# Attention units in pairs, a second tile of queries, and the fourth accumulator copy in another ring

## The chip, the cores and the metric

The kernel runs on one core of one Trainium2 chip. The metric is the device time of one execution in microseconds; shorter is better. Times are given as a median of several executions, and one more execution is recorded by the hardware profiler.

## The reference

The input is attention in chunks (batch 4, 8 heads, 768 positions, head dimension 64), whose output feeds two matrix layers. Cut to what matters:

```
chunk, left_ctx, right_ctx = 32, 16, 8           # every chunk also sees 8 memory keys
scores = (q_c @ k_full^T) / sqrt(64)             # per chunk, 64 keys
a      = exp(scores - max);  a = a / (sum(a) + 1e-9)
x      = a @ v_full                              # 3072 tokens x 512
x      = leaky_relu(x @ w_in, 0.01) @ w_out      # 512 -> 2048 -> 512   (first layer pair)
out    = ((x @ w_a) * (x @ w_b)) @ w_out2        # 512 -> 1536 -> 512   (second layer pair)
```

All data are float32. Each big product is three matmuls over parts: a factor is split into a rounded part (xh, gh, the first half of w) and the rest (xl, gl, the second half), and low by high, high by low and high by high are added up.

## The kernel before

The 3072 tokens are cut into 24 attention units of 128 tokens, and into six blocks of 512 tokens, so four units make a block. The list SEQ gives the order of the units.

One unit has these steps. Its scores are 32 matmuls of 64 columns into a PSUM tile s of the ring "s" (L279, function a_scores). ScalarE (ACT) places the queries of a later unit into the tile qz (L251, L252, q_place). VectorE (DVE) takes the maximum and subtracts it, ACT takes the exponential, DVE divides and transposes (L293 to L348). The product with V is 32 more matmuls of 64 columns into a tile pv of the same ring "s" (L388, a_pv). That ring has two buffers. The tile pv is then read: for units of blocks 0 to 3 by a_out, which casts it to xh on ACT (L421) and lets DVE subtract it again for xl (L422), and for units of blocks 4 and 5 by a_raw, which is one copy on ACT (L405 or L408).

Beside the attention runs the first layer pair, as items (block, f), where f is one of 16 slices of the hidden layer. One item is mm1 (12 matmuls of 512 columns into h, L435 to L437), leaky relu and split on ACT and DVE (g, gh, gl; L527, L530, L533), and mm2 of an earlier item (12 matmuls into the four accumulators a of the block, L559 to L563). After the last f of a block the four accumulators are copied by ACT to tiles x (the ring "z", three buffers) and stored to x2d (L576, L577). Blocks 4 and 5 follow in another form (products A, B, C with sums u and s in the rings "t" and "z"; their functions record all at L49). The second layer pair takes the rest of the time, from about 600 us.

A third strand prepares the weights of the second layer pair during blocks 1 to 3: raw words are loaded (raw<-w, L704), scaled by ACT (L106), joined by DVE (L116, L119), combined (ps, L755), split by ACT and DVE (tiles pwa and pwb, L125 and L126) and stored again (wab, wtd).

The order is fixed by hand and by the scheduler. The list STARTS holds, for each unit from the ninth on, the number of the item at which its scores are issued; its softmax, transposes and product with V follow at the next three items. The scheduler then fixes one order for each engine. Each engine works through its own order strictly, and SyncE (SP) issues the DMAs in its order. Weights w are loaded by wo_load into the ring "wo" of six buffers, which the second part of each item reads.

Of the kernel before, what the change touches and what calls it, by code (L numbers as in the profile page):

```python
# [7 lines left out]
F32 = mybir.dt.float32  # L8
# [6 lines left out]
P = 128  # L15
B, H, S, D = 4, 8, 768, 64
CH, LEFT, RIGHT, NMEM = 32, 16, 8, 8
WIN = LEFT + CH + RIGHT
UT = 128
# [7 lines left out]
TB = 512  # L27
NB3 = NT // TB
NL = NB3 - 2
SEQ = list(range(12)) + [16, 12, 13, 14, 15] + list(range(17, NU))  # L30


class InOrder:
# [22 lines left out]
def kernel(  # L56
# [144 lines left out]
    att = tc.tile_pool(name="att", bufs=4, side="left")  # L201
    ap_ = att.__enter__()
    ident = sm.tile([P, P], F32, tag="id", name="id", bufs=1)
    qz = ap_.tile([P, 16, 2 * CH], F32, tag="qz", name="qz", bufs=1)
    qs = [
        prep.tile([P, 2 * CH, 16], F32, tag=t, name="qs", bufs=1) for t in ("pz", "ps", "pwa", "pwb")
    ]
# [11 lines left out]
    for t in qs[2:4]:  # L219
        nc.gpsimd.memset(t[0:64, CH:2 * CH, :], 0.0)  # L220
        nc.gpsimd.memset(t[64:128, 0:CH, :], 0.0)
    nc.gpsimd.memset(qz[0:64, :, CH:2 * CH], 0.0)
    nc.gpsimd.memset(qz[64:128, :, 0:CH], 0.0)

    kt, vt, st, qr = {}, {}, {}, {}
    qu, ku, vu = [[a[u] for u in SEQ] for a in (q_l, k_l, v_l)]
# [3 lines left out]
    def q_load(upto):  # L230
        while loaded[0] < min(upto, NU):
            u = loaded[0]
            if u < len(qs):
                eng = act if u < 1 else sp
                sp.dma_start(out=qs[u][0:64, 0:CH, :], in_=qu[u][0:64])
                eng.dma_start(out=qs[u][64:128, CH:2 * CH, :], in_=qu[u][64:128])
            else:
                t = ap_.tile([P, CH, 16], F32, tag="qr", name="qr", bufs=2)
                sp.dma_start(out=t, in_=qu[u])
                qr[u] = t  # L240
            loaded[0] += 1

    def q_of(u):
        return qs[u].rearrange("p q o -> p o q") if u < len(qs) else qz

    def q_place(u, copy):
        if u >= NU:
            return
        t = qr.pop(u).rearrange("p q o -> p o q")
        qb = qz  # L250
        copy(qb[0:64, :, 0:CH], t[0:64])  # L251
        copy(qb[64:128, :, CH:2 * CH], t[64:128])  # L252

    def k_load(upto):
        while loaded[1] < min(upto, 2 * NU):
            u, cp = divmod(loaded[1], 2)
            t = ap_.tile([P, 512], F32, tag="k", name="k")
            sp.dma_start(out=t, in_=ku[u][cp])
            kt[u, cp] = t
            loaded[1] += 1  # L260
# [282 lines left out]
    def mm2(bi, parts, g):  # L543
        if bi not in acc:
            last = bi == NB3 - 1
            acc[bi] = [
                p.tile([P, TB], F32, tag=t, name="a")
                for p, t in (((ps_h, "h"), (ps_s, "s")) * 2 if last else ((ps_a, "a"),) * KC)
            ]
        gh, gl = g  # L550
        for o, n, f in parts:
            slot = wslot[f, 1]
            t = slice(o, o + n)
            for e in range(KC):
                ps = acc[bi][e][:, t]
                c = slice(e * P, e * P + P)

                kw = dict(skip_group_check=bi == 0)
                pe.matmul(  # L559
                    ps, slot[:, 1, c], gh[:, t], start=f == 0 and o == 0, stop=False, **kw  # L560
                )
                pe.matmul(ps, slot[:, 0, c], gl[:, t], start=False, stop=False, **kw)  # L562
                pe.matmul(  # L563
                    ps, slot[:, 0, c], gh[:, t], start=False,
                    stop=f == NF1 - 1 or (o == HALF and f == LEAD - 1), **kw
                )
            if bi == 0:
                ready = {(0, NF1 - 1): slice(0, HALF), (HALF, LEAD - 1): slice(HALF, TB)}
                t = ready.get((o, f))
            else:  # L570
                t = t if f == NF1 - 1 else None
            if t is not None:
                for e in range(KC):
                    ps = acc[bi][e][:, t]
                    y = tp.tile([P, TB], F32, tag="z", name="x2", bufs=3)
                    act.copy(y[:, t], ps)  # L576
                    (act if bi == NB3 - 1 else sp).dma_start(out=x2d[bi][:, e, t], in_=y[:, t])  # L577

# [96 lines left out]
    def at_item(i, *args):  # L675
        at(*divmod(i, NF1), *args)

    STARTS = (17, 20, 23, 26, 29, 32, 34, 37, 39, 42, 44, 47, 50, 52, 54, 57)
    for k, i in enumerate(STARTS):
        u = 2 * TB // UT + k  # L680
        blk, o = divmod(SEQ[u], TB // UT)
        at_item(i, a_scores, u)
        at_item(i, load_qk, u)
        at_item(i, a_soft1, u)
        at_item(i + 1, a_soft2, u)
        at_item(i + 2, a_turn, u)
        at_item(i + 3, a_pv, u, ps_s, "s")
        at_item(i + 3, load_v, u)
        if blk < NL:
            at_item(i + 3, a_out, u, ("x", blk), o * UT)  # L690
        else:
            at_item(i + 3, a_raw, u)

    sources = []
    for p in range(NF2 // 2):
# [151 lines left out]
    def wo_load(upto):  # L847
        while wo_next[0] < upto:
            b, f = 1 + wo_next[0] // NF1, wo_next[0] % NF1
            if b == NB3:  # L850
                break
            t = wop.tile([P, 2, 512], F32R, tag="wo", name="w")
            nc.sync.dma_start(out=t.bitcast(F32), in_=wod[f])
            wslot[f, 1] = t
            wo_next[0] += 1
# [95 lines left out]
            pe.matmul(ps, w[:, 0, c], lo[:, kc], start=False, stop=False, **kw)  # L951
            pe.matmul(ps, w[:, 0, c], hi[:, kc], start=False, stop=kc == hc - 1, **kw)

    at_item(max(STARTS) + 3, y_begin)
    at_item(max(STARTS) + 4, y_subs)
    at_item(max(STARTS) + 5, s_begin)

    STEPS = 58
    for bi, f, parts in items[LEAD:]:
        first = bi == 0  # L960
        if f == 0 and not first:
            if bi + 1 < NL:
                x_tiles(("x", bi + 1))
            else:
                x_raw()
        if first:
            W1.load(2 * f + 14)
            W1.step()
        behind.append((bi, parts, mm1(bi, parts)))
        if first:  # L970
            W1.step()
        if len(behind) > LAG:
            mm2(*behind.pop(0))
        for fn in beside.get((bi, f), []):
            fn()
        if not first:
            wo_load((bi - 1) * NF1 + f + 4)

            i = (bi - 1) * NF1 + f
            n = (NL - 1) * NF1  # L980
            for _ in range(STEPS * (i + 1) // n - STEPS * i // n):
                next(steps, None)
        elif f >= NF1 - 1:
            wo_load(f - NF1 + 2)
            prep_load(f - NF1 + 1)


    def relu(src, kept=None):
        g = tp.tile([P, TB], F32, tag="t", name="g")
        act.activation(g, src, AF.Prelu, alpha=0.01)  # L990
        if kept is None:
            gh = tp.tile([P, TB], F32R, tag="gh", name="gh", bufs=3)
            gl = tp.tile([P, TB], F32R, tag="gl", name="gl", bufs=3)
        else:
            w = wp.tile([P, 2, TB], F32R, tag=f"wi{kept}", name="g5")
            gh, gl = w[:, 0], w[:, 1]
        act.copy(gh, g)

        def low():
            dve.tensor_tensor(out=gl, in0=g, in1=gh.bitcast(F32), op=ALU.subtract)  # L1000
            return gh, gl

        return low
# [3 lines left out]
        act.copy(t, ps)  # L1007
        return t

    def summed(x, y):  # L1010
        t = tp.tile([P, TB], F32, tag="z", name="s", bufs=3)
        dve.tensor_tensor(out=t, in0=x, in1=y, op=ALU.add)
        return t

# [18 lines left out]
    for p in range(NF1 // 2):  # L1033
        f0, f1 = 2 * p, 2 * p + 1
        A = ps_h.tile([P, TB], F32, tag="h", name="A")
        prod(A, p, 0, 0, True)
        Bk = ps_s.tile([P, TB], F32, tag="s", name="B")
        if p:
            act.copy(Bk, A)
            low12 = relu(late, f1 - 2)  # L1040
        else:
            a1 = snapped(A)
            y_part(2)
        next2(behind.pop(0))
        if p:
            kept[f0 - 2] = low12()
        prod(Bk, p, 1, 1, p == 0)
        if p:
            next(steps, None)
        if p and p + 1 < NF1 // 2:  # L1050
            s_sums(p + 1)
        low11 = relu(Bk if p else summed(a1, Bk))
        g11 = low11()
        if not p:
            s_sums(p + 1)
        prod(A, p, 2, 4, False)
        u2 = snapped(A)
        if p == 0:
            y_part(6)
        C = ps_s.tile([P, TB], F32, tag="s", name="C")  # L1060
        prod(C, p, 3, 3, True)
        if p + 1 < NF1 // 2:
            s_parts(p + 1, 0)
            s_parts(p + 1, 1)
        prod(A, p, 4, 5, False)
        u3 = snapped(A)
        s22 = summed(u3, C)
        next2(part2(NL, f0, g11))
        kept[f1] = relu(s22, f0)()
        if p:  # L1070
            next(steps, None)
        prod(A, p, 5, 2, False)
        low21 = relu(A)
        prod(C, p, 6, 6, False)
        behind.append(part2(NL, f1, low21()))
        late = summed(u2, C)
# [520 lines left out]
```

## Time and profile before

| | us |
|---|---|
| three runs | 1123.5, 1125.94, 1125.79 |
| median of these | 1125.79 |
| profiled execution, its own time | 1122.23 |
| span of the profiled execution | 1120.4 |
| PE (TensorE) busy | 1099.6 |
| DVE busy | 774.0 |
| ACT busy | 527.1 |

The span is what the trace covers; the 1.8 us beside it in the profiled execution's own time lie around it. The three runs lie 2.4 us apart.

In the profile, PE is the matmul side of TensorE and PEld its weight loads. A row of the timeline gives the start, the duration, the engine and the line, the operation, and what is written and read; in square brackets stands how long the engine was idle just before and what released it.

### The profile page before, as it was taken

Reading aid. Unit: us, or ns where it says so; the run is one execution under the profiler, and the core shown is the slowest. Engines: PE = TensorE matmul, PEld = TensorE weight load, DVE = VectorE, ACT = ScalarE, POOL = GpSimd, SP = SyncE. Lnnn points to the kernel's source line nnn. Section 1 sums busy time; section 2 is a strip of 40 time slices with the busy share of each in tenths; the row PEclk is TensorE's granted clock in tenths of the full one; section 3 lists DMA queues with packets and bytes.
Section 4 is the critical chain, followed back from the end, with each engine's and each line's share of the span. In section 5 each row is a group of like instructions: output and inputs, shape, how many; then the busy total and the mean of one; then the engine's idle time right before and its main releaser. Section 6 shows DMA issues by size and latency. Waiting matters only on the chain.

```text
span 1120.4 us, 16313 instructions
## 1 busy us (share of the span) xinstructions
PE 1099.6 (98%) x6194; PEld 909.0 (81%) x6194; DVE 774.0 (69%) x1418; ACT 527.1 (47%) x893; POOL 6.3 (1%) x16
## 2 busy tenths in 40 slices
PE   7899999999999999999999999999999999999997
PEld 6788888888887887888888888888888888888886
DVE  6796489988997975777441737588736578745666
ACT  5887555465555535666522434144434243433232
POOL 2000000000000000000000000000000000000000
PEclk9999999999999999999999999999999999999999
DMA  9996789999998953444687756566877576867452
GB/s 312 404 349 228 280 330 325 337 319 312 345 316 312 343 189 132 155 147 141 206 335 248 271 186 206 172 212 196 272 227 222 167 225 190 241 179 244 142 187 76
DMA packets 100526, 271.15 MB, mean 242 GB/s; under 512 B 9696, under 2 KB 24672, under 8 KB 99680
## 3 DMA queue, kind: packets, MB, share of 16 engines
q1 hardware_dynamic: 98704, 268.41, 71.3%
q10 hardware_dynamic: 1744, 1.70, 0.5%
q8 instruction: 49, 0.80, 0.3%
q14 instruction: 29, 0.24, 0.1%
HBM read 215.29 MB, written 54.79 MB: 241 GB/s over the span
## 4 chain that ended last, share of the span: by engine, by line
PE 93%; issue 2%; ACT 2%; DVE 1%; DMA 1%; ACTq 0%; SPq 0%; DVEq 0%
PE ca L49 18%; PE cc L49 9%; PE oa L49 8%; PE a L49 7%; PE h L435 5%; PE h L436 5%; PE h L437 5%; PE a L559 5%; PE a L562 5%; PE a L563 5%; PE cb L49 5%; PE oy L49 4%; PE A L49 4%; PE pv L388 2%; PE C L49 2%
## 5 line engine op out<-in xcount | busy, mean ns | idle before, releaser
L49 PE MATMUL ca<-ch,wab 128*128 128x512 f32 x576 | 192.1, 389 | 0.1
L49 ACT CAST st<-gb 128x512 fp32r<-128x512 f32 x126 | 76.6, 622 | 124.5 <-DVE gb L49 123.9
L49 PEld LDWEIGHTS ca<-ch,wab 128*128 128x128 f32 x576 | 108.1, 188 | 23.3 <-ACT a L49 0.5
L49 PE MATMUL ca<-cl,wab 128*128 128x512 f32 x288 | 112.1, 389 | 0.0
L49 PE MATMUL oa<-st,wt 128*128 128x512 f32 x420 | 104.3, 389 | 0.0
L435 PE MATMUL h<-xh,w 128*128 128x512 f32 (+1 forms) x256 | 101.9, 398 | 0.7 <-ACT xh L49 0.7
L49 PE MATMUL cc<-ch,wab 128*128 128x512 f32 x288 | 100.3, 389 | 0.0
L436 PE MATMUL h<-xl,w 128*128 128x512 f32 (+1 forms) x256 | 98.7, 386 | 0.2 <-DVE xl L49 0.2
L559 PE MATMUL a<-gh,w 128*128 128x512 f32 (+1 forms) x256 | 97.7, 382 | 1.1 <-ACT x L576 1.1
L437 PE MATMUL h<-xh,w 128*128 128x512 f32 (+1 forms) x256 | 98.7, 385 | 0.0
L562 PE MATMUL a<-gl,w 128*128 128x512 f32 (+1 forms) x256 | 97.5, 381 | 0.0
L563 PE MATMUL a<-gh,w 128*128 128x512 f32 (+1 forms) x256 | 97.4, 381 | 0.0
L49 DVE TENSOR_TENSOR st<-gb,st 128x512 fp32r<-128x512 f32 x126 | 85.3, 689 | 14.9 <-ACT st L49 12.5
L49 PEld LDWEIGHTS oa<-st,wt 128*128 128x128 f32 x420 | 78.8, 188 | 16.4
L49 ACT COPY u<-ca 128x512 f32<-128x512 f32 x72 | 42.3, 587 | 91.5 <-PE ca L49 91.3
L348 DVE STREAM_TRANSPOSE pt<-p 32x128 f32<-32x128 f32 x256 | 77.5, 303 | 4.4
L49 PEld LDWEIGHTS cc<-ch,wab 128*128 128x128 f32 x288 | 54.0, 188 | 11.2
L49 PEld LDWEIGHTS ca<-cl,wab 128*128 128x128 f32 x288 | 54.0, 188 | 11.0
L435 PEld LDWEIGHTS h<-xh,w 128*128 128x128 f32 x256 | 48.1, 188 | 11.4 <-ACT xh L49 0.8
L559 PEld LDWEIGHTS a<-gh,w 128*128 128x128 f32 x256 | 48.1, 188 | 10.8 <-ACT x L576 1.5
L533 DVE TENSOR_TENSOR gl<-g,gh 128x512 fp32r<-128x512 f32 (+1 forms) x64 | 43.2, 675 | 18.5 <-ACT gh L530 14.9
L49 PE MATMUL cc<-cl,wab 128*128 128x512 f32 x144 | 56.0, 389 | 0.0
(197 smaller groups left out, 2035.8 us busy)
## 6 DMA issues: line engine op xcount, KB each, us to landing
wab<-wab SPq DMA_DIRECT2D x126, 512.0 KB, 4.4
w<-wod SPq DMA_DIRECT2D x80, 512.0 KB, 5.6
raw<-w SPq DMA_DIRECT2D x68, 512.0 KB, 7.0
wt<-wtd SPq DMA_DIRECT2D x63, 512.0 KB, 4.6
k<-kl SPq DMA_DIRECT2D x48, 256.0 KB, 5.2
v<-vl SPq DMA_DIRECT2D x48, 256.0 KB, 5.3
wab<-pwb SPq DMA_DIRECT2D x12, 768.0 KB, 7.1
wod<-w SPq DMA_DIRECT2D x16, 512.0 KB, 6.5
```

The lines of the kernel that those rows point to most:

```text
L49: self.last = emit(*args, **kwargs).ins
L348: dve.transpose(out=pt[o0:o0 + 32, :, 2 * cpar + hpar, hpx, :], in_=p[i0:i0 + 32, hpx::2, 32 * b:32 * b + 32],)
L388: pe.matmul(o[64 * hpar:64 * hpar + 64, 2 * pair:2 * pair + 2, t0:t0 + CH], v[:, i:i + 64], pt[:, 2 * cp + pair, 2 * cpar + hpar].rearrang ...
L435: pe.matmul(ps, w[1], x[0], start=first, stop=False)
L436: pe.matmul(ps, w[0], x[1], start=False, stop=False)
L437: pe.matmul(ps, w[0], x[0], start=False, stop=last)
L533: dve.tensor_tensor(out=gl[:, c], in0=g[:, c], in1=gh[:, c].bitcast(F32), op=ALU.subtract)
L559: pe.matmul(ps, slot[:, 1, c], gh[:, t], start=f == 0 and o == 0, stop=False, **kw)
L562: pe.matmul(ps, slot[:, 0, c], gl[:, t], start=False, stop=False, **kw)
L563: pe.matmul(ps, slot[:, 0, c], gh[:, t], start=False, stop=f == NF1 - 1 or (o == HALF and f == LEAD - 1), **kw)
```

## The change

Three things change. First, from the ninth unit on, the units go in pairs: the list STARTS has nine places instead of sixteen, and at each place the products with V of one pair are issued in a row, and then the scores of the next pair in a row. Units 16 and 17 of SEQ stand together. Second, a pair needs two tiles of queries: the second qz is taken from the ring "wo" that holds weights, which has five buffers left for weights while the attention runs, so a weight is asked for three items ahead instead of four. Third, for blocks after the first the fourth accumulator copy takes its buffer from the ring "t" and not from "z", and so does the first sum s.

```
-SEQ = list(range(12)) + [16, 12, 13, 14, 15] + list(range(17, NU))
+SEQ = list(range(12)) + [16, 17, 12, 13, 14, 15] + list(range(18, NU))
...
-    qz = ap_.tile([P, 16, 2 * CH], F32, tag="qz", name="qz", bufs=1)
+    qz = [ap_.tile([P, 16, 2 * CH], F32, tag="qz", name="qz", bufs=1)]
...
+    def q_tile(u):
+        return qz[u % 2 if u > 8 else 0]
...
-                    y = tp.tile([P, TB], F32, tag="z", name="x2", bufs=3)
+                    tag, bufs = ("z", 3) if e < KC - 1 or bi == 0 else ("t", None)
+                    y = tp.tile([P, TB], F32, tag=tag, name="x2", bufs=bufs)
...
-    STARTS = (17, 20, 23, 26, 29, 32, 34, 37, 39, 42, 44, 47, 50, 52, 54, 57)
-    for k, i in enumerate(STARTS):
-        u = 2 * TB // UT + k
+    def q_second():
+        qz.append(wop.tile([P, 16, 2 * CH], F32, tag="wo", name="qz"))
+        nc.gpsimd.memset(qz[1][0:64, :, CH:2 * CH], 0.0)
+        nc.gpsimd.memset(qz[1][64:128, :, 0:CH], 0.0)
+        q_place(9, nc.scalar.copy)
+        q_load(12)
+
+    def next_pair(u):
+        for k in (2, 3):
+            q_place(u + k, nc.scalar.copy)
+        q_load(u + 6)
+        k_load(2 * u + 8)
+
+    def out_of(u):
         blk, o = divmod(SEQ[u], TB // UT)
-        at_item(i, a_scores, u)
-        at_item(i, load_qk, u)
+        if blk < NL:
+            a_out(u, ("x", blk), o * UT)
+        else:
+            a_raw(u)
+
+    at(0, NF1 + LEAD - 1, q_second)
+    STARTS = (17, 23, 29, 34, 40, 45, 50, 55, 60)
+    for k, i in enumerate(STARTS[:-1]):
+        u, end = 2 * TB // UT + 2 * k, STARTS[k + 1]
+        for v in (u, u + 1):
+            at_item(end, a_pv, v, ps_s, "s")
+            at_item(end, out_of, v)
+        at_item(end, v_load, 2 * u + 8)
+    for k, i in enumerate(STARTS[:-1]):
+        u = 2 * TB // UT + 2 * k
+        for v in (u, u + 1):
+            at_item(i, a_scores, v)
+        at_item(i, next_pair, u)
         at_item(i, a_soft1, u)
+        at_item(i, a_soft1, u + 1)
         at_item(i + 1, a_soft2, u)
         at_item(i + 2, a_turn, u)
-        at_item(i + 3, a_pv, u, ps_s, "s")
-        at_item(i + 3, load_v, u)
-        if blk < NL:
-            at_item(i + 3, a_out, u, ("x", blk), o * UT)
-        else:
-            at_item(i + 3, a_raw, u)
+        at_item(i + 2, a_soft2, u + 1)
+        at_item(i + 3, a_turn, u + 1)
...
-            wo_load((bi - 1) * NF1 + f + 4)
+            wo_load((bi - 1) * NF1 + f + 3)
...
-    def summed(x, y):
-        t = tp.tile([P, TB], F32, tag="z", name="s", bufs=3)
+    def summed(x, y, tag="z"):
+        t = tp.tile([P, TB], F32, tag=tag, name="s", bufs=3 if tag == "z" else None)
...
-        low11 = relu(Bk if p else summed(a1, Bk))
+        low11 = relu(Bk if p else summed(a1, Bk, "t"))
```

Numbers behind an underscore tell buffers apart; lines of the changed kernel stand a few higher (a_pv L391, a_scores L282, a_out L424 and L425, the accumulator copies L580).

The order of PE in the kernel before, in the second block, where one unit's product with V (pv) ends and the next unit's scores (s) begin:

```order
L563 MATMUL a_1750<-gh_1948,w_1768 128x512
L388 MATMUL pv_2066<-pt1_130,v_1566 64x2x32 x8
L388 MATMUL pv_2066<-pt1_130,v_1568 64x2x32 x8
L279 MATMUL s_2089<-k_1712,qz_124 64x64 x8
L279 MATMUL s_2089<-k_1714,qz_124 64x64 x8
L435 MATMUL h_2129<-xh_375,w_852 128x512
L436 MATMUL h_2129<-xl_376,w_852 128x512
```

One product is followed by one score, and the score takes the buffer that the score before it left.

The order of PE in the changed kernel at the second pair of products, in the same block:

```order
L566 MATMUL a_1787<-gh_2351,w_2262 128x512
L391 MATMUL pv_2448<-pt0_129,v_2088 64x2x32 x8
L391 MATMUL pv_2448<-pt0_129,v_2090 64x2x32 x8
L391 MATMUL pv_2467<-pt1_130,v_2092 64x2x32 x8
L391 MATMUL pv_2467<-pt1_130,v_2094 64x2x32 x8
L438 MATMUL h_2561<-xh_375,w_1268 128x512
L439 MATMUL h_2561<-xl_376,w_1268 128x512
L440 MATMUL h_2561<-xh_375,w_1268 128x512
L282 MATMUL s_2494<-k_2138,qz_124 64x64 x8
L282 MATMUL s_2494<-k_2140,qz_124 64x64 x8
L282 MATMUL s_2511<-k_2142,qz_1607 64x64 x8
L282 MATMUL s_2511<-k_2144,qz_1607 64x64 x8
```

Two products and two scores stand together, with three matmuls of h between them. Both products take a buffer of the ring "s", and both scores take one after them.

The order of ACT in the kernel before at the same place of PE (xh<-pv is the reader of pv, raw and pwb belong to the preparation of the weights):

```order
L527 ACTIVATE g_2048<-h_2035 128x512
L530 CAST gh_2050<-g_2048 128x512
L125 CAST pwb_2234<-ps_2222 128x4x256
L421 CAST xh_1611<-pv_2066 128x4x128
L106 ACTIVATE raw_2124<-raw_2124 128x512
L251 COPY qz_124<-qr_1907 64x16x32
```

The cast of pv stands alone, behind a split of prepared weights.

The order of ACT in the changed kernel at that second pair:

```order
L530 ACTIVATE g_2430<-h_2417 128x512
L533 CAST gh_2432<-g_2430 128x512
L106 ACTIVATE raw_2607<-raw_2607 128x512
L424 CAST xh_1620<-pv_2448 128x4x128
L125 CAST pwa_2977<-pz_2780 128x256
L424 CAST xh_1620<-pv_2467 128x4x128
L125 CAST pwa_2977<-pz_2780 128x256 x2
```

A scaling of raw words now stands ahead of the first cast of pv, and a split of prepared weights between the two casts.

The order of DVE in the changed kernel there, with the second readers (xl<-pv):

```order
L116 TENSOR_SCALAR pz_2780<-raw_2607 128x512
L119 SCALAR_TENSOR_TENSOR pz_2780<-raw_2607,pz_2780 128x512
L783 TENSOR_TENSOR ps_2978<-pz_2780,ps_2978 128x256
L783 TENSOR_TENSOR ps_2978<-pz_2780 128x256
L425 TENSOR_TENSOR xl_1621<-pv_2448,xh_1620 128x4x128
L126 TENSOR_TENSOR pwa_2977<-pz_2780,pwa_2977 128x256
L425 TENSOR_TENSOR xl_1621<-pv_2467,xh_1620 128x4x128
```

A join (pz) and two sums (ps) stand ahead of the first subtraction, and a split of weights between the two.

The order of ACT in the kernel before at the end of block 2, where the accumulators a are copied (gh, in the last row but one, is for mm2):

```order
L576 COPY x2_3900<-a_2807 128x512
L576 COPY x2_3903<-a_2808 128x512
L576 COPY x2_3906<-a_2809 128x512
L125 CAST pwa_4315<-pz_4231 128x256 x3
L527 ACTIVATE g_3956<-h_3943 128x512
L530 CAST gh_3958<-g_3956 128x512
L576 COPY x2_3909<-a_2810 128x512
```

The fourth copy stands behind three splits and behind g and gh of the next item.

The order of ACT in the changed kernel at the end of block 2:

```order
L580 COPY x2_3897<-a_2805 128x512
L580 COPY x2_3900<-a_2806 128x512
L580 COPY x2_3903<-a_2807 128x512
L580 COPY x2_3906<-a_2808 128x512
L125 CAST pwb_4402<-ps_4269 128x4x256
L530 ACTIVATE g_3937<-h_3924 128x512
L533 CAST gh_3939<-g_3937 128x512
```

The four copies now stand in a row, ahead of the next split, g and gh.

## Rows read from the trace of the kernel before

**Rows 1.** The page: the span, and busy times and clock by engine.

```profile
span 1120.4 us, 16313 instructions
...
PE 1099.6 (98%) x6194; PEld 909.0 (81%) x6194; DVE 774.0 (69%) x1418; ACT 527.1 (47%) x893; POOL 6.3 (1%) x16
...
PEclk9999999999999999999999999999999999999999
```

**Rows 2.** Stage 135 to 245 us: length, busy of PE, PEld, DVE, ACT, POOL, clock, DMA.

```profile
135.00:245.00 110.00, 110.00 (x815) 91.24 (x814) 95.45 (x230) 63.31 (x102) 0.00 (x0) 1.00 0.92 320
```

**Rows 3.** What PE waited for, us in total, times, longest; two rows.

```profile
PE A L49 <- ACT u L49: 1.3, 1, 1.3
PE a L559 <- ACT x L576: 1.1, 1, 1.1
```

**Rows 4.** Timeline of PE around a pv and s run, and an s run.

```profile
153.85 0.39 PE L563 MATMUL a<-gh,w 128*128 128x512 f32 x1
154.17 1.15 PE L388 MATMUL pv<-pt,v 128*64 128x64 f32 x32
...
156.18 0.50 PE L435 MATMUL h<-xh,w 128*128 128x512 f32 x1
156.52 0.39 PE L436 MATMUL h<-xl,w 128*128 128x512 f32 x1
...
241.21 0.39 PE L563 MATMUL a<-gh,w 128*128 128x512 f32 x1
241.53 1.15 PE L279 MATMUL s<-k,qz 128*64 128x64 f32 x32
242.61 0.50 PE L435 MATMUL h<-xh,w 128*128 128x512 f32 x1
242.94 0.39 PE L436 MATMUL h<-xl,w 128*128 128x512 f32 x1
```

**Rows 5.** Timeline, all engines, at the first stall of PE.

```profile
342.13 0.39 PE L563 MATMUL a<-gh,w 128*128 128x512 f32 x1
...
342.95 0.59 ACT L576 COPY x<-a 128x512 f32<-128x512 f32 x1 [0.28 <-DMA x2d<-x]
...
343.59 0.50 PE L559 MATMUL a<-gh,w 128*128 128x512 f32 x1 [1.07 <-ACT x L576]
```

**Rows 6.** Timeline, all engines, at the second stall of PE.

```profile
437.80 0.58 ACT L49 COPY u<-A 128x512 f32<-128x512 f32 x1
...
438.44 1.65 PE L49 MATMUL A<-y,sw 128*128 128x512 f32 x6 [1.27 <-ACT u L49]
```

**Rows 7.** Timelines of three units: pv on PE, then its last reader.

```profile
191.29 1.15 PE L388 MATMUL pv<-pt,v 128*64 128x64 f32 x32
...
194.32 0.69 DVE L422 TENSOR_TENSOR xl<-pv,xh 128x512 fp32r<-128x512 f32 x1
...
280.33 1.15 PE L388 MATMUL pv<-pt,v 128*64 128x64 f32 x32
...
287.35 0.69 DVE L422 TENSOR_TENSOR xl<-pv,xh 128x512 fp32r<-128x512 f32 x1
...
324.57 1.15 PE L388 MATMUL pv<-pt,v 128*64 128x64 f32 x32
...
325.76 0.59 ACT L408 COPY x<-pv 128x512 f32<-128x512 f32 x1 [0.46 <-PE pv L388]
```

**Rows 8.** Waits of ACT, 36 to 600 us; DMA issues, 136 to 345 us.

```profile
ACT raw L106 <- DMA raw<-w: 29.6, 14, 4.8
...
raw<-w SPq DMA_DIRECT2D x21, 512.0 KB, 6.9
```

**Rows 9.** Groups of ACT and DVE, 136 to 345 us, by form.

```profile
L106 ACT ACTIVATE raw<-raw 128x512 f32<-128x512 f32 x22 | 14.8, 675 | 26.1 <-DMA raw<-w 25.8
...
L119 DVE SCALAR_TENSOR_TENSOR pz<-raw,pz 128x512 int32<-128x512 int32 x22 | 15.2, 691 | 0.6
```

More of the change, by code (lines that the diff above doesn't have):

```diff
@@ L221 @@
         nc.gpsimd.memset(t[64:128, 0:CH, :], 0.0)
-    nc.gpsimd.memset(qz[0:64, :, CH:2 * CH], 0.0)
-    nc.gpsimd.memset(qz[64:128, :, 0:CH], 0.0)
+    nc.gpsimd.memset(qz[0][0:64, :, CH:2 * CH], 0.0)
+    nc.gpsimd.memset(qz[0][64:128, :, 0:CH], 0.0)
     kt, vt, st, qr = {}, {}, {}, {}
@@ L241, in q_load @@
             loaded[0] += 1
+    def q_tile(u):
+        return qz[u % 2 if u > 8 else 0]
     def q_of(u):
-        return qs[u].rearrange("p q o -> p o q") if u < len(qs) else qz
+        return qs[u].rearrange("p q o -> p o q") if u < len(qs) else q_tile(u)
     def q_place(u, copy):
@@ L249, in q_place @@
         t = qr.pop(u).rearrange("p q o -> p o q")
-        qb = qz
+        qb = q_tile(u)
         copy(qb[0:64, :, 0:CH], t[0:64])
@@ L952, in prod @@
             pe.matmul(ps, w[:, 0, c], hi[:, kc], start=False, stop=kc == hc - 1, **kw)
-    at_item(max(STARTS) + 3, y_begin)
-    at_item(max(STARTS) + 4, y_subs)
-    at_item(max(STARTS) + 5, s_begin)
+    at_item(max(STARTS), y_begin)
+    at_item(max(STARTS) + 1, y_subs)
+    at_item(max(STARTS) + 2, s_begin)
     STEPS = 58
```

## The prediction

> **What bounds the kernel now.** I read the page first. PE is busy 1099.6 us of a span of 1120.4 us and holds its full clock in every slice; DVE and ACT are busy 774 and 527 us [rows 1]. The table of busy times by stage says the same where the change works: in the 110 us from 135 to 245 us PE is busy all the time, at a clock of 1.00 (2.4 GHz), while DVE has some 15 us free and ACT 47 us [rows 2]. So the time of the kernel is the sum of what PE issues plus the few places where it waits. The list of waits of PE then shows that there is little to win by removing waits: behind the first item of block 0 only two are above 1 us, 1.3 us for ACT's copy u and 1.1 us for ACT's copy x [rows 3]. A change can shorten this kernel by these two waits or by making PE's own stream cheaper, and can lengthen it by any new wait of PE. I therefore went through the change with one question: what does PE issue, and what does it newly wait for?
>
> **Fewer switches between narrow and wide matmuls.** The order of PE holds as many matmuls as before. What changes is how often 64-column matmuls stand between 512-column ones. A 512-column matmul follows another at 0.227 us. In the timeline the stretch from the start of the last wide matmul ahead of a pv and s run (153.85) to the start of the second one behind it (156.52) is 2.67 us; without the run it would be two steps, 0.45 us, so the run of 64 adds 2.215 us. A run of 32 adds 1.73 - 0.45 = 1.28 us in the same way (241.21 to 242.94) [rows 4]. The difference, 0.93 us for 32 matmuls, is 29.2 ns each, so 0.35 us of every run are not matmuls but the switch in and out. From the ninth unit on the order has 22 such runs before and 13 in the changed kernel: 9 x 0.35 = **-3.1 us**. No row shows a run of 128; I take its switch for the same. The bounds are -3.1 and, if a switch grew with the run, nothing.
>
> **The fourth copy.** At 342 us PE ends its accumulation in 342.13, and the next matmul starts at 343.59, since the fourth copy x ran only from 342.95: its row shows it waiting for the store x2d of an earlier x, whose buffer of the ring "z" it needed [rows 5]. Normal spacing would have been 0.23 us, so the stall is about 1.25 us, and 0.1 us more at the slower first step behind it. In the changed order the four copies stand in a row, ahead of a split and of g and gh, and the item's mm2 that needs the accumulators comes over 2 us later. I take **-1.35 us**; it is bounded by 0, if the first copy itself is late. At 438 us the stall is of the same kind, 1.27 us of idle and 0.28 us of slower steps, behind ACT's copy u, which had begun at 437.80 [rows 6]. The copy of A now takes a buffer of "t" in competition with x, s, g and u, so it waits for an older user of that ring (the subtraction gl). I take half, **-0.7 us**, between 0 and -1.55.
>
> **The second tile of queries.** Two memsets on POOL, which is nearly idle (6.3 us in all, [rows 1]), and 2 placing copies that ACT makes anyway. The weights w are asked for three items ahead, 3 x 5.44 us (24 steps of 0.227 us), so about 16 us: far longer than any landing in the list of DMA issues (6.9 us for raw words of the same 512 KB, [rows 8]). Nothing, both ways. Its cover is that distance; if the queue were a whole item late, there would still be about 4 us.
>
> **Two products and two scores in one ring of two.** This is the part that costs. In the order of PE at the second pair, pv, pv take both buffers of the ring "s"; then come three matmuls of h, and the two scores, which must have the same two buffers. So s waits until pv has been read, by ACT's cast xh and DVE's subtraction xl (units of blocks 2 and 3) or by ACT's copy x (blocks 4, 5). Before, s took the buffer that another score had left long ago, and the reader of pv could be late without anyone waiting.
>
> How late is it? Three units bound it. The reader xl ended 3.7 us after pv had started (191.29 to 194.32 + 0.69) in the quickest of eight units, and 7.7 us after it in the slowest (280.33 to 287.35 + 0.69); the copy ended after 1.8 us where ACT was free (324.57 to 325.76 + 0.59) [rows 7]. I took the same distance for all sixteen units between 154 and 410 us: the eight with xl have a mean of 5.0 us, the eight with a copy a mean of 2.6 us (1.8 to 4.9). The distance is long because ACT and DVE work in a strict order and other work stands ahead of the readers: in 36 to 600 us ACT waited 29.6 us for raw words, 14 times and up to 4.8 us, and these land 6.9 us after their issue [rows 8]. The changed order keeps that: at the second pair a scaling of raw words stands ahead of the first xh, a split pwa between the two casts, and on DVE a join and two sums ahead of xl.
>
> When does PE want the buffer? From the start of pv a run of 64 lasts 2.0 us until the next wide matmul starts (154.17 to 156.18, [rows 4]), and M wide matmuls between products and scores bring it to about 2.2 + 0.23 M us; with M = 0 it is 1.9 us. The order has seven places where two products are followed by two scores. Four are units with xl, with M of 2, 3, 7 and 2: a mean distance of 5.0 gives stalls of 2.4, 2.1, 1.2 and 2.4 us. Three are units with a copy and M = 0: 2.6 - 1.9 = 0.7 us each. The sum is 8.1 + 2.1 = 10.2 us. Stepping through each place by hand in the new order, with raw words landing 6.9 us after an issue that stands some 5 us ahead of pv, I come to a little less, 9.4 us. At the second pair this goes: raw lands 1.9 us after pv's start, scaled at 2.6 (0.675), joined at 3.7 (about 0.42 and 0.69), two sums to 4.5, xl to 5.2 us [rows 9], where the score wants it at 2.9; so 2.3 us, and up to 0.8 us more for the second score behind the split. I take **+9.4 us**. The bounds: with the quickest distances, 3.7 and 1.8, the four places give 1.1 + 0.8 + 0 + 1.1 = 3 us; with the slowest, 7.7 and 4.9, they give 18 us and the copies 9.
>
> The Trainium skill, "Perfetto Trace Analysis", section on optimizing TensorE's matmuls, asks for independent matmul groups to rotate through different PSUM banks so that the evacuation of one overlaps the next group's matmuls. In the kernel before a product and the next score do rotate in that way, and by rows 7 the evacuation of 3.7 to 7.7 us is hidden; the pairs use up the rotation. If the rule's overlap survived the pairing, the sum would be -5.2 us; without it, it is +4.2 us.
>
> **Sum:** -3.1 - 1.35 - 0.7 + 9.4 = +4.2 us. The profiled execution took 1122.23 us by its own time (span 1120.4), so it would take 1126.5 us. That execution lies 3.6 us below the median of the runs, so on the median, 1125.79, I forecast **1130 us**, slower by 0.37%. About 0.2%, 2.25 us, is what a measurement of this kernel can tell from no change.
>
> **The rivals.** *The readers are in time.* With nothing ahead of it, the reader on ACT starts 1.19 us after pv's start (324.57 to 325.76, [rows 7]); with 0.59 for a cast like that copy and 0.69 for xl, xl has ended 2.5 us after pv's start: just before the score wants it at the places with M of 2 or more, and the copies, at 1.8 us, cost nothing. For it speaks that a pair asks for the prepared weights in other items, so that raw words may have landed; against it that not one of eight units before came below 3.7 us. With 0 to 2 us of stalls left, the sum is -5.2 to -3.2 us, about **1121.5 us**, faster. It decides from stalls below 3 us in sum. *Half of it.* The readers are as quick as the quickest unit before, 3.7 us: stalls of some 3 to 6 us, the sum -2 to +1 us, **1125 us**, no change to be told. *Late words or a lower clock.* Raw words landing later (PE waits longer, so the queue behind it moves too), or the clock falling to 1.2 GHz in a stall of some 3 us. For it: the slowest unit, 7.7 us, and that no row shows such a long wait in this part of the kernel; against it: PE idled 1.27 us at 438 us with the clock at its full level after it [rows 1, 6]. Each wide matmul at the lower clock would take 0.23 us more; 20 of them cost 4.5 us. With 14 to 18 us of stalls or drops, the sum is +9 to +13 us, about **1137 us**.
>
> **How the numbers follow.** I give the forecast and its neighbourhood (+2.3 to +8 us) 0.47, the late case 0.13, half of it 0.18, and the readers in time 0.22. So slower has 0.60, the same 0.18, faster 0.22. The range reaches from the readers in time to the start of the late case, 1121.5 to 1136 us; if the kernel is slower, then by 1128 to 1134 us.
>
> **What would show it.** In the changed profile PE should wait for xl (DVE) or x, xr (ACT) in front of s, at seven places, about 1 to 3 us each, in a stretch from 170 to 410 us; the waits of ACT for raw words should stand just before them. The wait of a on x at 343 us should be gone, and the one of A on u should be shorter. Runs of 128 narrow matmuls should cost 0.35 us plus 29 ns a piece. The prediction is wrong if the waits for s sum to under 7 us, if PE's clock shows a slice under full, or if PE waits in the mm1 or mm2 of an item for weights w or gl.

## The result and the profile after

The changed kernel takes 1137.58 us (median of four runs, 1136.63 to 1138.41), the kernel before 1124.84 us (median of four, 1123.5 to 1125.94). The ratio is 1.0117, with a 95% interval of 1.0102 to 1.0132: slower by some 13 us. The forecast said slower, but 1130 us, and its range ended at 1136 us. The profiled execution took 1138.41 us by its own time, with a span of 1136.6 us, so it is 16.2 us longer in span than the profiled one before; the two executions that were profiled lie at the far ends of their kernels, and the ledger below is of these two.

The page of the changed kernel, the lines that answer to [rows 1]:

```profile
span 1136.6 us, 16339 instructions
...
PE 1103.5 (97%) x6194; PEld 916.4 (81%) x6194; DVE 773.1 (68%) x1418; ACT 527.2 (46%) x893; POOL 7.4 (1%) x18
...
PEclk9999999999999999999999999999999999999999
```

PE works 4 us longer for the same 6194 matmuls, and the rest of the 16 us is waiting. The slices of the clock row are 28 us each and hide what a shorter stretch shows. The same stage as in [rows 2], from the table of busy times by stretch:

```profile
135.00:245.00 110.00, 104.69 (x725) 87.21 (x724) 91.99 (x223) 57.13 (x91) 0.00 (x0) 0.97 0.85 298
```

PE, which was never idle there, is idle for 5.3 of 110 us, and its granted clock is 0.97 on the mean, where it was 1.00. The list of what PE waited for, which answers to [rows 3] (us in total, times, longest):

```profile
PE s L282 <- DVE xl L425: 7.6, 3, 3.6
...
PE s L282 <- ACT xr L408: 5.2, 2, 2.7
PE a L562 <- ACT x L580: 1.3, 1, 1.3
...
PE A L49 <- ACT u L49: 0.8, 1, 0.8
```

The first two rows are new: scores wait for the readers of pv, at five places, 12.8 us in sum. One such place, the first pair, in the timeline of all engines:

```profile
173.98 2.08 PE L391 MATMUL pv<-pt,v 128*64 128x64 f32 x64
...
176.14 0.67 ACT L106 ACTIVATE raw<-raw 128x512 f32<-128x512 f32 x1 [0.81 <-DMA raw<-w]
...
176.71 0.56 ACT L424 CAST xh<-pv 128x512 fp32r<-128x512 f32 x1
176.84 0.43 DVE L116 TENSOR_SCALAR pz<-raw 128x512 int32<-128x512 int32 x1 [0.74 <-ACT raw L106]
177.31 0.69 DVE L119 SCALAR_TENSOR_TENSOR pz<-raw,pz 128x512 int32<-128x512 int32 x1
...
177.92 0.68 DVE L425 TENSOR_TENSOR xl<-pv,xh 128x512 fp32r<-128x512 f32 x1
...
178.65 3.64 PE L282 MATMUL s<-k,qz 128*64 128x64 f32 x64 [1.93 <-DVE xl L425]
```

The reader xh stands behind a scaling of raw words that waited for its DMA, xl behind the join that follows it, and PE starts the scores 0.05 us after xl has ended. Then the 64 matmuls of the scores take 3.64 us where the 64 of the products took 2.08 us. The table by stretch says why (its last columns are the granted clock, the DMA share and GB/s):

```profile
177.50:178.60 1.10, 0.00 (x0) 0.00 (x0) 1.10 (x3) 0.82 (x2) 0.00 (x0) 1.00 1.06 402
178.75:179.75 1.00, 1.00 (x20) 1.00 (x22) 0.99 (x3) 0.16 (x1) 0.00 (x0) 0.50 1.03 397
181.00:182.00 1.00, 1.00 (x25) 1.00 (x22) 1.00 (x3) 0.99 (x2) 0.00 (x0) 0.50 0.49 182
182.50:183.50 1.00, 1.00 (x6) 0.78 (x6) 0.55 (x2) 0.97 (x3) 0.00 (x0) 1.00 0.00 0
```

When PE came back from 1.93 us of idling, the clock fell to 0.50, which is 1.2 GHz, and stayed there until about 182 us. The wait was paid a second time.

Not every place is like this one. The longest wait is at the fifth pair, and no DMA is waited for there:

```profile
318.44 2.09 PE L391 MATMUL pv<-pt,v 128*64 128x64 f32 x64
...
321.31 1.07 ACT L424 CAST xh<-pv 128x512 fp32r<-128x512 f32 x2
...
323.07 1.02 DVE L126 TENSOR_TENSOR pwa<-pz,pwa 128x512 fp32r<-128x512 f32 x2
324.01 1.28 DVE L425 TENSOR_TENSOR xl<-pv,xh 128x512 fp32r<-128x512 f32 x2
...
324.75 3.10 PE L282 MATMUL s<-k,qz 128*64 128x64 f32 x64 [3.56 <-DVE xl L425]
```

From the start of pv to the end of the first xl DVE is busy for 6.15 of 6.26 us, with joins, sums, splits and gl ahead of xl, and ACT idles 0.4 us in sum, each time for DVE. So here plain work stands ahead of the reader. At the first two pairs it is both: ACT idled up to 0.81 and 3.13 us for raw words, and the joins followed. At the sixth and seventh it is mostly the wait for a DMA: 2.57 us for raw words and 2.56 us for a store stand ahead of a copy.

**Where 16 us come from.** Both traces hold the same wide matmuls in the same sequence, so each can be matched with its counterpart, and every change in the distance from one to the next has a place:

| term | forecast, us | trace, us |
|---|---|---|
| 22 runs of narrow matmuls become 13 | -3.1 | -3.1 |
| fourth copy at 343 us | -1.35 | -1.35 |
| copy u at 438 us and the steps up to 456 us | -0.7 | -1.2 |
| seven pairs: PE idle in front of scores | +9.4 | +12.8 |
| the same places: narrow and wide matmuls at the lower clock, restarts | 0 | +6.6 |
| fourth copy of block 0, at 146 us | 0 | +1.5 |
| first 16 us, ahead of everything that changed | 0 | +1.0 |

The sum is 16.2 us. The seven places one by one, idle and lost clock together: 3.6, 3.7, 0, 0, 5.1, 2.7 and 4.3 us. The last row differs from run to run in other kernels too (from -0.6 to +1.1 us by the first 26 us in the traces of the experiments), so it is not put down to the change.

### The profile page after: what moved, and what is told of

Its sections match the earlier page's. It is cut to its first block, busy times and chain, and to the rows that moved or that the text cites. A ratio compares the mean times of both kernels' runs of the same rounds, so it can differ in the third digit from the quotient of the medians.

```text
span 1136.6 us, 16339 instructions
## 1 busy us (share of the span) xinstructions
PE 1103.5 (97%) x6194; PEld 916.4 (81%) x6194; DVE 773.1 (68%) x1418; ACT 527.2 (46%) x893; POOL 7.4 (1%) x18
## 4 chain that ended last, share of the span: by engine, by line
PE 81%; DVE 6%; DMA 4%; ACT 4%; issue 3%; SPq 1%; ACTq 0%; DVEq 0%
PE ca L49 18%; PE cc L49 9%; PE oa L49 8%; PE a L49 6%; PE cb L49 5%; PE oy L49 4%; PE h L438 4%; PE A L49 3%; PE h L440 3%; PE h L439 3%; PE a L562 3%; PE a L565 3%; PE a L566 3%; DMA raw<-w 2%; DVE pt L351 2%
## 5 line engine op out<-in xcount | busy, mean ns | idle before, releaser
L530 ACT ACTIVATE g<-h 128x512 f32<-128x512 f32 (+1 forms) x64 | 37.4, 585 | 44.6 <-PE h L440 44.3
```

What stands on the lines that cost most here:

```text
L530: act.activation(g[:, c], ps[:, c], AF.Prelu, alpha=0.01)
```

## The experiments

The theory after the result (A): the readers of pv are late because in the strict order of ACT and DVE the preparation's scalings and splits stand ahead of them and wait for DMA; pairs turn that into waits of PE, since two products take both buffers. The rivals: the amount of work ahead, landed or not, or pairs that bunch too much work in one place (B); the second tile of queries, the ring of five weight buffers and a crowded DMA queue (C). Comparisons are with the kernel before, run beside them on the same chip (its median 1123.66 to 1123.77 us there).

**The ring change alone**, on the kernel before:

```diff
-                    y = tp.tile([P, TB], F32, tag="z", name="x2", bufs=3)
+                    tag, bufs = ("z", 3) if e < KC - 1 or bi == 0 else ("t", None)
+                    y = tp.tile([P, TB], F32, tag=tag, name="x2", bufs=bufs)
...
-        low11 = relu(Bk if p else summed(a1, Bk))
+        low11 = relu(Bk if p else summed(a1, Bk, "t"))
```

> The kernel before with only the ring change (fourth accumulator copy and first sum in ring t). If the ring change is worth what the ledger of PE's steps says, the stall of 1.35 us at 343 us goes and the one at 438 us shrinks by 0.7 to 1.3 us: 2 to 2.7 us faster than before, about 1122.5 us. Rival: the waits only move into ring t and nothing is won, 1124 to 1126 us.

Measured 1120.54 us, ratio 0.9972 (0.9961 to 0.9982): 3.1 us faster. The stall of [rows 5] is gone, and the one of [rows 6] has shrunk to 0.8 us:

```profile
PE A L49 <- ACT u L49: 0.8, 1, 0.8
```

This part does what it says. By the two traces it is worth 1.35 us at the first stall and 1.2 us at the second, together half a microsecond more than forecast. The medians differ by more than that; the run of the second tile alone, below, shows what may lie behind it.

**Pairs without the ring change**, the changed kernel with that edit undone:

> The changed kernel without its ring change (pairs and second tile of queries only). The ring change alone won 3.1 us; if it wins the same among pairs, this is 2 to 4 us slower than the changed kernel, 1139.5 to 1142 us. Rival: among pairs the fourth copy is not on PE's path, and the time is that of the changed kernel within 1 us, 1136.5 to 1138.5 us.

Measured 1138.18 us, ratio 1.0123 (1.0101 to 1.0146). Against the changed kernel's ratio of 1.0117 that is no difference that the intervals can tell, nearer to the rival. Its trace says why: the stall at 343 us is gone here too, as pairs alone already change what ACT does at the end of that block, and the wait for u at the end of block 3 is 1.9 us where the changed kernel has 0.8 us. By these waits the ring change is worth about 1 us among pairs, where it won 3.1 us alone; the times exclude neither that nor 3 us. The -1.35 us of the table can't be given to it alone.

**The second tile of queries alone**, units still one by one:

```diff
+    def q_tile(u):
+        return qz[u % 2 if u > 8 else 0]
...
+        qz.append(wop.tile([P, 16, 2 * CH], F32, tag="wo", name="qz"))
...
-            wo_load((bi - 1) * NF1 + f + 4)
+            wo_load((bi - 1) * NF1 + f + 3)
```

> The kernel before with only the second tile of queries out of the ring of weights (two memsets more, weights asked for three items ahead), units still one by one. Theory A and B: within 1.5 us of the kernel before, 1122 to 1126 us. Rival C, five weight buffers and the shorter distance are part of the loss: 1127 us or more, with PE waiting for w.

Measured 1123.25 us, ratio 1.0000 (0.9991 to 1.0009). Rival C is out: the tile, the five buffers and the shorter distance cost nothing that the interval can tell, as the prediction had it, and no row has PE waiting for w. The traced execution took 1126.13 us, the longest of the twelve, and shows something else:

```profile
PE a L562 <- ACT x L579: 2.7, 2, 2.5
```

The stall of [rows 5], again behind the fourth copy, is 2.5 us here and not 1.1 us, and the clock is at 0.50 behind it. Nine of the twelve runs lie between 1122.1 and 1124.5 us and three between 1125.9 and 1126.1 us. So this stall, longer in some executions than in others, may also part the runs of the kernel before (1122.24 to 1127.42 us) and explain why the ring change, whose runs lie between 1119.5 and 1121.2 us, wins more than [rows 5] show. That is not shown: the kernel before was traced once.

**Raw words loaded one step earlier** in the changed kernel:

```diff
-    AHEAD = 3
+    AHEAD = 4
```

> The changed kernel with raw words loaded one step earlier (four ahead instead of three, as many as there are buffers). Theory A, the readers of pv are late because ACT waits for raw words to land: the waits of ACT for raw words shrink, the stalls of s at the first, second and sixth pair (3.6, 3.7 and 2.7 us with what the clock adds) fall to half or less, 1129 to 1133 us. Rival B, the readers are late because of the amount of other work that stands ahead of them in the order, landed or not: within 2 us of the changed kernel, 1135 to 1140 us.

Measured 1126.32 us, ratio 1.0022 (1.0009 to 1.0034): 11 us of the 13 are back from one number, more than either theory had put it. What PE still waited for:

```profile
PE s L282 <- DVE xl L425: 6.5, 4, 3.6
...
PE s L282 <- ACT xr L408: 0.9, 1, 0.9
```

The waits fell from 12.8 to 7.4 us, and only the one of 3.6 us lowered the clock; those of 0.8 to 1.1 us did not, and their scores ran at full speed. Two signs of theory A did not come, at least in the traced execution (1128.5 us, one of the longer of twelve that reach from 1123.77 to 1129.56 us). At the second pair the wait grew, from 2.1 to 3.6 us. And the waits of ACT for raw words fell by little, from 35.0 us in the changed kernel to 32.8 us here (36 to 600 us, two kernels, so two fences):

```profile
ACT raw L106 <- DMA raw<-w: 35.0, 15, 6.9
```

```profile
ACT raw L106 <- DMA raw<-w: 32.8, 17, 5.2
```

So this moved the waits away from the pairs more than it removed them: in the new order of ACT the scaling at the first pair, for one, comes behind the first xh instead of ahead of it. It shows that the loss hangs on what stands ahead of the readers, but does not part A from B.

**The same on the kernel before with the ring change**, units one by one:

> The ring change on the kernel before, with raw words loaded one step earlier. Theory A: ACT's waits for raw words shrink but nobody waited behind them while scores had a free buffer, so within 1 us of the ring change alone, 1119.5 to 1121.5 us. Rival: earlier words help any order, 1117 us or less.

Measured 1120.74 us, ratio 0.9972 (0.9961 to 0.9983), the same as without it. Here, where no score waited behind them, earlier words did not help.

**The products one item ahead of the scores** that take their buffers, so that 24 wide matmuls stand between them instead of 0 to 7:

```diff
-            at_item(end, a_pv, v, ps_s, "s")
-            at_item(end, out_of, v)
-        at_item(end, v_load, 2 * u + 8)
+            at_item(end - 1, a_pv, v, ps_s, "s")
+            at_item(end - 1, out_of, v)
+        at_item(end - 1, v_load, 2 * u + 8)
```

> The changed kernel with the two products of a pair issued one item (24 wide matmuls, 5.4 us) ahead of the two scores that take their buffers. Theory A, the loss is the ring of two buffers with readers 2 to 6 us late: the waits of s vanish and the clock stays full, 19 us less, and 4 more switches between narrow and wide matmuls cost 1.4 us: 1118 to 1122 us, faster than the kernel before. Rival C, the loss comes from the second tile of queries, the ring of five weight buffers or the crowded DMA queue: 1130 us or more.

Measured 1129.69 us, ratio 1.0058 (1.0042 to 1.0073): by the ratios some 7 us better than the changed kernel, and 8 us above the top of what theory A expected, so that the time alone does not part it from rival C (1130 us or more). The waits of s went down to 2.4 us as they should, but others came:

```profile
PE a L562 <- ACT x L580: 2.6, 1, 2.6
PE s L282 <- DVE xl L425: 2.4, 2, 1.6
PE pv L391 <- DVE pt L351: 2.1, 2, 1.7
```

The longest is at the end of block 1, in the timeline:

```profile
243.74 0.62 ACT L125 CAST pwa<-pz 128x512 fp32r<-128x512 f32 x1 [6.10 <-DMA wtd<-pwa]
...
244.75 0.58 ACT L580 COPY x<-a 128x512 f32<-128x512 f32 x1
...
245.38 0.50 PE L562 MATMUL a<-gh,w 128*128 128x512 f32 x1 [2.59 <-ACT x L580]
```

A split of prepared weights held ACT for 6.1 us, until a store had left its buffer, and the accumulator copies queued behind it. The readers of pv are only one of several things that stand behind the preparation on ACT. The transposes (pt) were late for products that now came an item earlier. No wait is for w, as rival C would have it.

**The same, with the second queries placed one item later:**

> The same, with the queries of the pair's second unit placed one item later. If the new stall of 1.5 us at 146 us is ACT's fourth accumulator copy standing behind four placements of queries in a row, it goes, and this is 1 to 2 us faster than the products one item ahead alone. Rival: the copy waits for a buffer of ring z, and the time is the same within 0.5 us.

Measured 1130.23 us, ratio 1.0063 (1.0048 to 1.0078), the same. The run told nothing on its question: the stall at 146 us was not there in the kernel it was to be compared with, and the order of ACT at that place is the same in both.

**Both: products an item ahead and raw words a step earlier:**

> The changed kernel with both the products one item earlier and raw words one step earlier. Theory A: the remaining waits of s (2.4 us) go, but the transposes for the last pair and the accumulator copies at 245 us are late for other reasons, 1123 to 1128 us, 2 to 6 us below the products one item earlier alone. Rival B, bunching: within 2 us of it, 1128 to 1132 us.

Measured 1120.11 us, ratio 0.9968 (0.9956 to 0.9980), faster than the kernel before, and lower than either theory had put it; one wait of s of 1.0 us is left. That speaks against B in the form "pairs bunch too much work": the work is all still there, though a pair's products and the scores now stand an item apart.

**The readers first.** All work is kept; only the order changes. Preparation steps of the two items ahead of a pair are done after it, and what ACT does for the preparation is queued behind the pair's last reader:

```diff
-            for _ in range(STEPS * (i + 1) // n - STEPS * i // n):
-                next(steps, None)
+            if i + NF1 + 1 not in STARTS[1:] and i + NF1 + 2 not in STARTS[1:]:
+                for _ in range(STEPS * (i + 1) // n - taken[0]):
+                    next(steps, None)
+                taken[0] = STEPS * (i + 1) // n
...
-        act.copy(hi[:, :, off:off + UT], o)
+        reader[0] = act.copy(hi[:, :, off:off + UT], o)
...
-        w_bias(raws[n])
+        with tc.issue_after(reader[0].ins):
+            w_bias(raws[n])
...
-        act.copy(hi, z)
+        with tc.issue_after(reader[0].ins):
+            act.copy(hi, z)
```

> The changed kernel with every scaling and split of the weight preparation that comes after a pair's products held behind that pair's last reader of pv on ACT; the preparation steps of the two items ahead of a pair are done after it. Nothing is left out. Theory A, the loss is that readers of pv stand behind the preparation's waits for DMA: the waits of s fall from 12.8 us to under 2 us, the clock stays full, 1118 to 1123 us, faster than the kernel before. Rival B, pairs bunch so much work on ACT and DVE that something else becomes late (accumulator copies, transposes for pv): the waits of s go but others of 4 us or more come, 1124 to 1131 us.

Measured 1118.52 us, ratio 0.9954 (0.9943 to 0.9966): by the ratios some 18 us below the changed kernel, and 5.1 us below the one before. The first pair again, in the timeline:

```profile
172.26 2.08 PE L392 MATMUL pv<-pt,v 128*64 128x64 f32 x64
...
173.46 0.59 ACT L425 CAST xh<-pv 128x512 fp32r<-128x512 f32 x1 [2.56 <-PE pv L392]
174.07 0.69 DVE L426 TENSOR_TENSOR xl<-pv,xh 128x512 fp32r<-128x512 f32 x1 [2.45 <-ACT xh L425]
174.27 0.50 PE L439 MATMUL h<-xh,w 128*128 128x512 f32 x1
174.39 0.59 ACT L425 CAST xh<-pv 128x512 fp32r<-128x512 f32 x1 [0.35 <-PE pv L392]
...
174.93 2.09 PE L283 MATMUL s<-k,qz 128*64 128x64 f32 x64
```

ACT and DVE now wait for PE, and xl has ended at 174.76, 2.5 us after pv's start; the score follows without a gap and at full speed. No row of PE's waits has s behind xl, x or xr any more, and in the table by stretch the clock is 1.00 from 135 to 440 us:

```profile
135.00:440.00 305.00, 302.96 (x2211) 251.49 (x2210) 253.16 (x601) 163.83 (x261) 0.00 (x0) 1.00 0.83 298
```

ACT's waits for raw words (36 to 600 us), 35.0 us in the changed kernel, have all but gone:

```profile
ACT raw L106 <- DMA raw<-w: 2.2, 1, 2.2
```

The same pairs, tile and ring, with two buffers: the loss came from what stood ahead of the readers. B in the form of bunched work falls, as all the work is there and no new wait of 4 us came. The other form of B, work ahead of the readers whether its words have landed or not, is not parted from A by this run, which moved the scalings that wait and the steps that only work alike. By the trace of the changed kernel both count: waits for a DMA at four of the five places, and work alone at the one with the longest wait.

**The second queries and the scalings also behind the last accumulator copy:**

```diff
-        for k in (2, 3):
-            q_place(u + k, nc.scalar.copy)
+        q_place(u + 2, nc.scalar.copy)
+        with tc.issue_after(xcopy[0].ins):
+            q_place(u + 3, nc.scalar.copy)
...
-        with tc.issue_after(reader[0].ins):
+        with tc.issue_after(reader[0].ins), tc.issue_after(last.ins):
```

> The readers' kernel (preparation held behind the last reader of pv), with the placing of the second queries and the scalings also held behind the last accumulator copy. If the stall at the end of block 0 (1.5 us in the changed kernel, 0.8 us with readers first) is ACT's fourth copy standing behind four placements in a row, it goes: 0.5 to 1 us faster than readers first, about 1117.7 us. If that copy waits for its buffer of ring z, the time is the same within 0.3 us.

Measured 1117.78 us, ratio 0.9942 (0.9929 to 0.9955), 0.7 us below the readers first by the medians, which is less than the two intervals are wide. The trace says more: the stall at the end of block 0 is gone, no row of PE's waits has a behind x any more. In the changed kernel it reads, in the timeline,

```profile
141.05 1.11 ACT L254 COPY qz<-qr 64x512 f32<-64x512 f32 x1
142.17 1.10 ACT L255 COPY qz<-qr 64x512 f32<-64x512 f32 x1
...
143.30 1.07 ACT L254 COPY qz<-qr 64x512 f32<-64x512 f32 x1
...
144.38 1.04 ACT L255 COPY qz<-qr 64x512 f32<-64x512 f32 x1
145.44 0.37 ACT L580 COPY x<-a 128x256 f32<-128x256 f32 x1
...
145.87 0.50 PE L562 MATMUL a<-gh,w 128*128 128x512 f32 x1 [1.27 <-ACT x L580]
```

with the copies of two units' queries in a row ahead of the fourth accumulator copy, which starts with no idle time before it, so it waited for no buffer of ring z. Since this run moved the scalings as well as the placing, it does not say which of the two took the stall away. This is the fastest version that ran, 6 us below the kernel before.

## Why the prediction was wrong

The direction was right, and so was the mechanism of the waits. The step that failed is the term "+9.4 us" for two products and two scores in one ring of two: it measured 19.4 us, 12.8 us of waits and 6.6 us of slower matmuls behind them.

**The waits themselves** were 3.4 us more than forecast, 12.8 us against 9.4. They came at five of the seven places, not at all seven. The four places with xl were well met in sum: expected 2.4, 2.1, 1.2 and 2.4 us, found 1.9, 2.1, 0 and 3.6, though the last of these came from work and not from late words. The error sits in the three with a copy, where I took a mean distance of 2.6 us and got 0.7 us of stall each; two of them waited 2.5 and 2.7 us. The mean mixed units with nothing ahead of the copy (1.8 us) with those behind a scaling or a split; in the new order the scaling stood between the two copies of one pair and a split that waited for a store ahead of the other. The order had it, and the mean hid it. (The bound for the slowest readers, given as 18 us, comes to 18.8 us by its own figures; nothing hangs on it.)

**The clock** was set to nothing in the sum and named only in a rival of 0.13, which is the case that came: 14 to 18 us of stalls and drops were written there, 1137 us, and 19.4 us came. The argument against it was that PE had idled 1.27 us with the clock at its full level after it [rows 6]. That says nothing of 2 to 4 us. Four of the five waits were followed by a clock of 0.50 for some 3 us, at about 1.6 us each (at the first place 64 narrow matmuls took 3.64 us and not 2.08).

**The block boundary** at 146 us was in no term. The placing of queries was priced as copies that ACT makes anyway; that is so, but two units' worth now stand in a row, 4.3 us, and one of PE's accumulators waited behind them. They are not the whole cause. In the trace of the pairs without the ring change ACT has the same order there, but had waited 1.66 us for raw words shortly before and not 2.83 us, and PE lost only 0.3 us.

**What held.** The nine fewer switches gave -3.1 us to a tenth, and a run of 128 pays one switch as a run of 64 does. The sum without stalls was -5.2 us, as in the first rival, and by the medians the readers-first kernel is 5.1 us below the kernel before. That the two agree to 0.1 us is partly luck: the two traces lie 3.7 us apart in span, with 0.9 us lost at the block boundary, which no term had, and a wait for u of 1.4 us that is not shorter than before. The same two buffers suffice when the readers are not held up. The reader's shortest distance of 2.5 us is met there as well. The rule of the Trainium skill, "Perfetto Trace Analysis" (matmuls), on rotating through PSUM banks so that the evacuation of one group overlaps the next group's matmuls, spoke rightly against the pairs as they were scheduled: in their trace scores waited 12.8 us for the evacuation.

## What to carry to other kernels

When work is grouped so that both buffers of a ring are taken at once, price the reader that frees them by what stands ahead of it in its engine's strict order and by what that waits for, place by place in the new order, not by a mean over the old one. A wait of the busiest engine can cost twice, once as idle time and once as the slower clock behind it; add the second as soon as a wait passes what the trace has shown to be harmless. And before giving up such a change, move the readers to the front of their queue: here that turned 13 us of loss into 5 us of gain.

## What the runs showed of the hardware

The length of a wait alone does not say whether the clock falls. In the changed kernel it fell behind waits of 1.93, 2.11, 3.56 and 2.68 us, and not behind one of 2.51 us, which lay between two halves of a run of scores:

```profile
357.16 1.10 PE L282 MATMUL s<-k,qz 128*64 128x64 f32 x32
360.77 1.15 PE L282 MATMUL s<-k,qz 128*64 128x64 f32 x32 [2.51 <-ACT xr L408]
```

The second half took 1.15 us, and the clock in the table by stretch is 1.00 for both the wait and what followed:

```profile
358.40:360.70 2.30, 0.00 (x0) 0.00 (x0) 0.42 (x1) 1.10 (x3) 0.00 (x0) 1.00 0.99 381
360.80:361.80 1.00, 1.00 (x32) 0.98 (x32) 1.00 (x2) 0.99 (x2) 0.00 (x0) 1.00 1.03 387
```

In the traces of the experiments, from 20 us on, waits of PE of up to 1.85 us left the clock at 1.00, and it fell in or behind each of those of 1.91 us and more. Why the one of 2.51 us did no harm stays open; no run was made for it.
